# Where the small scale products stand in a shared PSUM tile: behind the first-layer product instead of in front of it

## The chip, the cores and the metric

One core of a Trainium2 chip runs the kernel. The metric is device time in microseconds (us), the median of several runs; lower is better. The engines are TensorE (PE: matmuls; PEld: its weight loads), VectorE (DVE), ScalarE (ACT), GpSimd (POOL) and SyncE (SP), which issues the DMAs. Matmul results land in PSUM, which has eight banks of 512 float32 values for each of 128 partitions.

## The reference

Attention with a mask by hash buckets makes a matrix `x` of 1536 tokens by 512. After that come two feed-forward parts. The change lies in these, so they are what must be seen:

```python
# part 1: four experts, x is 1536x512, w1 4x512x1024, w2 4x1024x512
p = probs / (probs.sum(-1, keepdims=True) + 1e-9)
for e in range(4):
    out += p[:, e:e+1] * (np.maximum(x @ w1[e], 0) @ w2[e])
# part 2: w_in 512x2048, w_out 2048x512
h = out @ w_in
g = np.where(h >= 1, h, np.where(h <= -1, 0, (h + 1) ** 2 / 4))
return g @ w_out
```

The inputs `w_in` and `w_out` are float64; all others are float32.

## The kernel before

**Units, jobs, steps.** The hidden columns of both parts are cut into 12 units `u` of 512: units 0 to 7 are the experts (two units each), 8 to 11 are part 2. A job is a unit with a group of token tiles (128 tokens each), nearly always three tiles, so 384 columns; only the first four jobs of the stage looked at here have two tiles. A job has four steps `f`, one for each 128 of its hidden columns. A step has a first-layer product (`l1b`) and a second-layer part (`l2b`).

The product takes 12 matmuls into columns 0 to `n` (256 or 384) of one PSUM tile `mm`: both operands are split into a high and a low half in float16, and three of the four cross terms are summed over four chunks of 128 (lines 1314 to 1316). The tile fills one bank, and there are two such buffers (tag `m`), so that a buffer comes up again two products later. The second-layer part multiplies the job's tokens, tile by tile, into output tiles `o` (nine matmuls of 512 columns, lines 1341 to 1343), which live in the other six banks, two sets of three. In the fourth step VectorE adds them to `acc` (line 1356 or 1362; in unit 8 ScalarE copies them, line 1360).

**The evictions.** For units 0 to 7 ScalarE reads the product (`gg`, line 1320), makes its high half (`hh`, line 1321), and VectorE makes the low half (`hl`, line 1322). For units 8 to 11 ScalarE reads the product first (`ga`, line 1328), VectorE works on that (line 1329), reads the product again (`gg`, line 1330), ScalarE makes `hh` (line 1331) and VectorE makes `hl` (line 1332).

**The order of the work** in this stage (from about 451 us on) is the order in which the code below issues it. Each engine works off its own queue in that order. The main loop (lines 1427 to 1434) issues the product of job `j + 1`, step `f`, then `step()`, then the second-layer part of job `j`, step `f`, then `step()` again. So the results of a product are used by a second-layer part four steps later. `step()` moves on the side work by one piece each: scans for the largest magnitude of weight tiles (line 1072), the split of weight tiles into halves with their scale (`conv_w`, lines 1191 to 1196), and the bit operations that turn float64 weights into float32 (lines 1137 to 1150). `x_all` (line 1263) rebuilds an input tile in float16 and takes a PSUM tile of tag `m` for itself.

**The riders.** A scale is a power of two from the largest magnitude of a tensor. The largest value has to cross partitions, which TensorE does in two small products (`fin`, line 1078). The first kind, `turn_over`, transposes a column `mx` into one row of 128 (line 1086); VectorE takes the maximum of it (line 1087) and three more operations on single values give `dg` (lines 1088, 1076, 1090). The second kind, `spread`, multiplies `dg` with a row of ones (line 1095), and VectorE copies the result and its reciprocal (lines 1096, 1097). Both use columns 384 to 511 of a PSUM tile that a product uses as well: `rider(ps)` (line 1061) pops at most one of them for each product, when its age (one or two products) is up. Before the change it is called right after the tile is taken, ahead of the product's matmuls.

There are 52 riders, 26 of each kind. In the seven stretches that the rows below are given for, the counts are 3, 29, 8, 8, 2, 2 and 0. The first stretch has the last eight products of 256 columns; the second has the seven units with two jobs each (56 products); each of the five others is one unit with four jobs (16 products): the last expert unit, then units 8 to 11. Three input tiles are rebuilt in the third and nine in the fourth.

Of the kernel before, what the change touches and what calls it, by code (L numbers as in the profile page):

```python
# [285 lines left out]
def attn_moe_kernel(ctx: ExitStack, tc, q, k, v, proj, probs, w1, w2, w_in, w_out, out):  # L286
# [484 lines left out]
    def x_tiles(tt):  # L771
        return x_t[tt // 6], (tt % 6) * 128
# [66 lines left out]
    def l1_mm(j, f, ps, kcs):  # L839
        u, tts = jobs[j]  # L840
        n = 128 * len(tts)
        (xh, xl), c0 = x_tiles(tts[0])
        hi, lo = wt[1][4 * job_load[j] + f]
        for kc in kcs:
            ws = slice(kc * 128, kc * 128 + 128)
            xs = slice(c0, c0 + n)
            pe.matmul(ps[:, 0:n], hi[:, ws], xh[:, kc, xs], start=(kc == 0), stop=False)  # L847
            pe.matmul(ps[:, 0:n], hi[:, ws], xl[:, kc, xs], start=False, stop=False)  # L848
            pe.matmul(ps[:, 0:n], lo[:, ws], xh[:, kc, xs], start=False, stop=(kc == KC - 1))  # L849

    def l1_hi(j, f, ps):
        n = 128 * len(jobs[j][1])
        hts[j, f] = [mode["h"].tile([128, mode["hn"]], F32R, tag=f"h{x}", name=f"h{x}") for x in "hl"]
        act.activation(hts[j, f][0][:, 0:n], ps[:, 0:n], AF.Relu)

    def l1_lo(j, f, ps):
        n = 128 * len(jobs[j][1])
        hh, hl = hts[j, f]
        dve.scalar_tensor_tensor(hl[:, 0:n], ps[:, 0:n], 0.0, hh[:, 0:n].bitcast(F32), ALU.max, ALU.subtract)
# [94 lines left out]
    with tc.manual_schedule():  # L954
# [103 lines left out]
        def mm_tile():  # L1058
            return ps_m.tile([128, 512], F32, tag="m", name="mm")

        def rider(ps):
            for x in pend:
                x[0] -= 1
            if pend and pend[0][0] <= 0:
                pend.pop(0)[1](ps[:, 384:512])
# [161 lines left out]
        def need(kind, u, f):  # L1227
            while (kind, u, f) not in w16:
                got = next(wgen[kind])
                if got is False:  # L1230
                    raise RuntimeError(f"weights {kind} {u} {f} too early")
                if got == "fin" and pend:
                    pend.pop(0)[1](mm_tile()[:, 384:512])
                if got == "w64":
                    next(w64)
# [45 lines left out]
        def scales2(u, c):  # L1281
            if u not in k5:
                k5[u] = t_p.tile([128, 5, 4], F32, tag="k5", name="k5")
            k2, kh, gp, cc, ko = (k5[u][:, i, c] for i in range(5))
            dve.tensor_scalar(k2, e2[:, c], ew[1, u], None, ALU.mult)
            dve.tensor_scalar(kh, k2, 0.5, None, ALU.mult)
            dve.tensor_scalar(gp, k2, 2.0 ** 15, 2.0 ** -15, ALU.mult, ALU.max)
            dve.reciprocal(cc, gp)
            dve.tensor_scalar(ko, gp, ew[2, u], None, ALU.mult)

        def grp(j):
            return jobs[j][1][0] // 3

        def l1b(j, f):
            u, tts = jobs[j]
            n = 128 * len(tts)
            if j >= JF:
                need(1, u, f)
            ps = mm_tile()
            rider(ps)  # L1300
            seen[1].add((j, f))
            if j < JF:
                l1_mm(j, f, ps, range(KC))
                l1_hi(j, f, ps)
                l1_lo(j, f, ps)
                return
            b, c0 = tts[0] // 6, (tts[0] % 6) * 128
            assert all(x_done.count(tt) == (tt >= 6) + (u >= 8) for tt in tts), (j, u, tts, f, x_done, J0, turn)
            xh, xl = x16[b]
            hi, lo = w16[1, u, f]  # L1310
            for kc in range(KC):
                ws = slice(kc * 128, kc * 128 + 128)
                xs = slice(c0, c0 + n)
                pe.matmul(ps[:, 0:n], hi[:, ws], xh[:, kc, xs], start=(kc == 0), stop=False)  # L1314
                pe.matmul(ps[:, 0:n], hi[:, ws], xl[:, kc, xs], start=False, stop=False)  # L1315
                pe.matmul(ps[:, 0:n], lo[:, ws], xh[:, kc, xs], start=False, stop=(kc == KC - 1))  # L1316
            hts[j, f] = hh, hl = [h_p.tile([128, 256], F32R, tag=f"h{y}", name=f"h{y}").bitcast(F16) for y in "hl"]
            gg = g_p.tile([128, 384], F32, tag="gg", name="gg")
            if u < 8:
                act.activation(gg[:, 0:n], ps[:, 0:n], AF.Relu, scale=2.0 ** -15)  # L1320
                act.activation(hh[:, 0:n], gg[:, 0:n], AF.Copy)  # L1321
                dve.tensor_tensor(hl[:, 0:n], gg[:, 0:n], hh[:, 0:n], ALU.subtract)  # L1322
            else:
                if f == 0 and (u == 8 or grp(j) == 0):
                    scales2(u, slice(grp(j), grp(j) + 1) if u == 8 else slice(0, 4))
                k2, kh, gp, cc, ko = (k5[u][:, i, grp(j):grp(j) + 1] for i in range(5))
                a = g_p.tile([128, 384], F32, tag="ga", name="ga")
                act.activation(a[:, 0:n], ps[:, 0:n], AF.Relu, bias=half, scale=kh)  # L1328
                dve.scalar_tensor_tensor(a[:, 0:n], a[:, 0:n], 1.0, a[:, 0:n], ALU.min, ALU.mult)  # L1329
                dve.scalar_tensor_tensor(gg[:, 0:n], ps[:, 0:n], k2, a[:, 0:n], ALU.mult, ALU.max)  # L1330
                act.activation(hh[:, 0:n], gg[:, 0:n], AF.Copy, scale=cc)  # L1331
                dve.scalar_tensor_tensor(hl[:, 0:n], gg[:, 0:n], cc, hh[:, 0:n], ALU.mult, ALU.subtract)  # L1332
# [92 lines left out]
        for f in range(4):  # L1425
            l1b(J0, f)
        for j in range(J0, J1 - 1):
            for f in range(4):
                l1b(j + 1, f)
                if turn and (f or j > JF):  # L1430
                    x_all(*turn.pop(0))
                step()
                l2b(j, f)
                step()
            if jobs[j][0] == LB[NA0]:
                x2q.append(x2_steps(jobs[j][1]))
# [31 lines left out]
```

## Time and profile before

| what | value |
|---|---|
| runs | 1214.49, 1215.84, 1219.51 us; median 1215.84 |
| the profiled execution | 1216.15 us, its span 1214.4 us |
| mean granted clock of TensorE | 0.93 |
| PE, PEld busy | 1024.3 us (84%), 634.8 us (52%) |
| DVE, ACT, POOL busy | 765.3 us (63%), 685.7 us (56%), 287.1 us (24%) |

The span goes from the first to the last instruction of one execution; the rest of the execution's time lies around it. Busy time is the time in which an engine had an instruction of its own at work. Matmuls overlap in their pipeline: one of 512 columns is recorded at some 0.38 us, while the next starts 0.22 us after it, so the distance of starts is what a matmul costs. The granted clock is the share of the full TensorE clock (2.4 GHz) that was granted; it has two levels, 1.0 and 0.5, and other values are means.

### The profile page before, as it was taken

Reading aid. Unit: us, or ns where it says so; the run is one execution under the profiler, and the core shown is the slowest. Engines: PE = TensorE matmul, PEld = TensorE weight load, DVE = VectorE, ACT = ScalarE, POOL = GpSimd, SP = SyncE. Lnnn points to the kernel's source line nnn. Section 1 sums busy time; section 2 is a strip of 40 time slices with the busy share of each in tenths; the row PEclk is TensorE's granted clock in tenths of the full one; section 3 lists DMA queues with packets and bytes.
Section 4 is the critical chain, followed back from the end, with each engine's and each line's share of the span. In section 5 each row is a group of like instructions: output and inputs, shape, how many; then the busy total and the mean of one; then the engine's idle time right before and its main releaser. Section 6 shows DMA issues by size and latency. Waiting matters only on the chain. (4 is left out here: it accounts for less than half of the span.)

```text
span 1214.4 us, 19439 instructions
## 1 busy us (share of the span) xinstructions
PE 1024.3 (84%) x6897; PEld 634.8 (52%) x6897; DVE 765.3 (63%) x2059; ACT 685.7 (56%) x1497; POOL 287.1 (24%) x333
## 2 busy tenths in 40 slices
PE   7589998898999986688778788888877796987998
PEld 3257886686888874344334344444433453443554
DVE  7898888887898565444444543334555666574655
ACT  7888887888788445545445445443543453333332
POOL 0324655345565541101101101120110020000000
PEclk7689999999999988889898889899988999998999
DMA  8999999989999554221312210001100101100002
GB/s 208 209 163 200 214 221 245 212 152 205 188 181 169 126 174 136 70 87 53 104 52 76 61 55 18 1 18 35 35 18 18 35 19 35 35 1 0 1 27 79
DMA packets 252146, 119.40 MB, mean 98 GB/s; under 512 B 180624, under 2 KB 237328, under 8 KB 252048
## 3 DMA queue, kind: packets, MB, share of 16 engines
q1 hardware_dynamic: 249792, 116.84, 42.7%
q10 hardware_dynamic: 2256, 1.31, 0.6%
q8 instruction: 54, 0.88, 0.3%
q14 instruction: 44, 0.36, 0.1%
HBM read 68.19 MB, written 3.15 MB: 59 GB/s over the span
## 5 line engine op out<-in xcount | busy, mean ns | idle before, releaser
L1322 DVE TENSOR_TENSOR hl<-gg,hh 128x384 f16<-128x384 f32 (+1 forms) x80 | 44.6, 557 | 224.1 <-ACT hh L1321 224.1
L683 POOL TENSOR_TENSOR pn<-e,pn 128x192 f16<-128x192 f32 (+3 forms) x157 | 127.9, 819 | 192.7 <-DVE pn L683 54.0
L1320 ACT ACTIVATE gg<-mm 128x384 f32<-128x384 f32 (+1 forms) x80 | 38.3, 478 | 191.1 <-PE mm L1316 191.1
L1314 PE MATMUL mm<-x161h,w1l 128*128 128x384 f16 x192 | 67.6, 352 | 44.8 <-DVE mt L1087 31.5
L1314 PE MATMUL mm<-x161h,w1h 128*128 128x384 f16 x192 | 67.4, 351 | 43.6 <-DVE mt L1087 30.7
L655 DVE CUSTOM_DVE_ANT_0 e<-s,mk,sc 128x768 f32<-128x768 f32 x96 | 96.8, 1008 | 2.7 <-ACT acc L713 1.3
L1331 ACT ACTIVATE hh<-gg,k 128x384 f16<-128x384 f32 x64 | 39.3, 615 | 102.0 <-DVE gg L1330 102.0
L668 ACT ACTIVATE e<-e,usm 128x768 f32<-128x768 f32 x96 | 89.3, 931 | 3.4 <-POOL w1l L833 0.4
L633 PE MATMUL s<-xk,xq 128*128 128x384 f16 (+1 forms) x384 | 83.7, 344 | 8.6 <-DVE usm L655 8.1
L1329 DVE SCALAR_TENSOR_TENSOR ga<-ga 128x384 f32<-128x384 f32 x64 | 40.5, 633 | 75.8 <-ACT ga L1328 75.8
L675 ACT ACTIVATE pn<-e 128x768 f16<-128x768 f32 (+3 forms) x121 | 85.1, 703 | 2.8 <-DMA pt<-pn 2.1
L1328 ACT ACTIVATE ga<-mm,half,k 128x384 f32<-128x384 f32 x64 | 42.5, 665 | 75.4 <-PE mm L1316 66.6
L1341 PE MATMUL o<-w2l,hh 128*128 128x512 f16 x216 | 84.2, 390 | 0.0
L1342 PE MATMUL o<-w2l,hh 128*128 128x512 f16 x216 | 83.5, 386 | 0.0
L847 PE MATMUL m<-x0h,w1h 128*128 128x256 f32 x272 | 83.1, 305 | 0.1
L1343 PE MATMUL o<-w2l,hl 128*128 128x512 f16 x216 | 82.7, 383 | 0.0
L1341 PE MATMUL o<-w2h,hh 128*128 128x512 f16 x208 | 82.4, 396 | 0.0
L1342 PE MATMUL o<-w2h,hh 128*128 128x512 f16 x208 | 81.5, 392 | 0.0
L1343 PE MATMUL o<-w2h,hl 128*128 128x512 f16 x208 | 80.2, 386 | 0.0
L848 PE MATMUL m<-x0l,w1h 128*128 128x256 f32 x272 | 76.8, 283 | 0.0
L849 PE MATMUL m<-x0h,w1l 128*128 128x256 f32 x272 | 76.8, 282 | 0.0
L1315 PEld LDWEIGHTS <-w1h 128*128 128x128 f16 x288 | 29.9, 104 | 88.8 <-issue 73.7
(255 smaller groups left out, 2948.0 us busy)
## 6 DMA issues: line engine op xcount, KB each, us to landing
raw<-in_moe_w_dram SPq DMA_DIRECT2D x123, 256.0 KB, 3.6
r<-in_moe_w_in_dram SPq DMA_DIRECT2D x16, 512.0 KB, 3.8
rawx<-in_moe_w_dram SPq DMA_DIRECT2D x32, 256.0 KB, 4.0
r<-in_moe_w_out_dram SPq DMA_DIRECT2D x16, 512.0 KB, 3.6
out_dram<-acc SPq DMA_DIRECT2D x12, 256.0 KB, 2.1
rk<-in_k_dram SPq DMA_DIRECT2D x5, 384.0 KB, 3.9
rv<-in_v_dram SPq DMA_DIRECT2D x5, 384.0 KB, 4.6
pt<-pn SPq DMA_TRANSPOSE x96, 4.2
```

Of the source, the lines that this page charges most:

```text
L633: pe.matmul(sps[:, j, 0:n], st["xq"][1 - i][:, hh * QG[pgs[m][0]][2] + c], st["x"][:, hh, 384 * j:384 * j + n], start=(i == 0), stop=(i == 1))
L655: dve.tensor_tensor_reduce(out=e.rearrange("p (a b) -> p a b", a=2), in0=u["s"][:, :, 0:384], in1=u["mk"].rearrange("p (a b) -> p a b", a= ...
L668: act.activation(u["e"], u["e"], AF.Exp, scale=-1.0, bias=sm[:, 2:3], accum_out=sm[:, 3:4])
L675: act.activation(u["pn"][:, c0:c1], u["e"][:, c0:c1], AF.Copy)
L683: eng[e].tensor_tensor(u["pn"][:, 768 + c0:768 + c1], u["e"][:, c0:c1], u["pn"][:, c0:c1], ALU.subtract)
L847: pe.matmul(ps[:, 0:n], hi[:, ws], xh[:, kc, xs], start=(kc == 0), stop=False)
L848: pe.matmul(ps[:, 0:n], hi[:, ws], xl[:, kc, xs], start=False, stop=False)
L849: pe.matmul(ps[:, 0:n], lo[:, ws], xh[:, kc, xs], start=False, stop=(kc == KC - 1))
L1314: pe.matmul(ps[:, 0:n], hi[:, ws], xh[:, kc, xs], start=(kc == 0), stop=False)
L1341: pe.matmul(o, hh[:, ts], whi, start=(f == 0), stop=False)
L1342: pe.matmul(o, hh[:, ts], wlo, start=False, stop=False)
L1343: pe.matmul(o, hl[:, ts], whi, start=False, stop=(f == 3))
```

## The change

The call of `rider(ps)` moves from the front of the product to its end. In the branch for the first two jobs of the stage (`j < JF`) it goes between the product and the two evictions; in the general branch it goes behind the loop over `kc` and ahead of the first instruction that evicts the tile.

```diff
             ps = mm_tile()
-            rider(ps)
             seen[1].add((j, f))
             if j < JF:
                 l1_mm(j, f, ps, range(KC))
+                rider(ps)
                 l1_hi(j, f, ps)
                 l1_lo(j, f, ps)
                 return
...
                 pe.matmul(ps[:, 0:n], lo[:, ws], xh[:, kc, xs], start=False, stop=(kc == KC - 1))
+            rider(ps)
             hts[j, f] = hh, hl = [h_p.tile([128, 256], F32R, tag=f"h{y}", name=f"h{y}").bitcast(F16) for y in "hl"]
             gg = g_p.tile([128, 384], F32, tag="gg", name="gg")
```

## Rows read from the trace of the kernel before

**Rows 1.** The page, part 1: busy time, share of the span, instructions.

```profile
PE 1024.3 (84%) x6897; PEld 634.8 (52%) x6897; DVE 765.3 (63%) x2059; ACT 685.7 (56%) x1497; POOL 287.1 (24%) x333
```

**Rows 2.** Waits of PE over the span: us in total, times, longest.

```profile
PE mm L1314 <- DVE mt L1087: 73.7, 26, 5.9
PE mm L1314 <- DVE sw L1097: 30.0, 22, 4.3
...
PE mm L1314 <- DVE gg L1330: 9.1, 6, 4.0
...
PE mm L1086 <- DVE mx L1083: 7.9, 5, 2.6
...
PE mm L1314 <- DVE s L1097: 7.0, 4, 2.2
```

**Rows 3.** Instruction groups, 500 to 1215 us: count | busy us, mean ns | idle before.

```profile
L776 PE MATMUL mm<-ident,acc 128*128 128x128 f32 x48 | 8.7, 312 | 0.0
```

**Rows 4.** Seven stretches: length, PE, PEld, DVE, ACT, POOL busy, granted clock, DMA.

```profile
451.30:492.90 41.60, 26.77 (x159) 18.78 (x159) 25.77 (x55) 22.72 (x55) 4.95 (x5) 0.89 0.51 150
492.90:805.00 312.10, 250.99 (x1193) 124.85 (x1193) 138.83 (x338) 149.66 (x322) 38.00 (x32) 0.89 0.18 55
805.00:884.40 79.40, 69.28 (x356) 35.83 (x356) 37.13 (x90) 35.07 (x73) 8.21 (x8) 0.96 0.09 28
884.40:984.80 100.40, 76.88 (x382) 40.35 (x380) 58.42 (x140) 43.58 (x80) 9.50 (x8) 0.92 0.07 22
984.80:1064.60 79.80, 67.08 (x339) 34.25 (x338) 51.18 (x95) 34.14 (x61) 9.42 (x7) 0.94 0.11 33
1064.60:1140.30 75.70, 65.83 (x340) 33.56 (x338) 47.31 (x89) 29.02 (x50) 6.95 (x6) 0.95 0.00 1
1140.30:1202.60 62.30, 62.30 (x338) 32.90 (x337) 36.99 (x66) 20.47 (x32) 0.00 (x0) 1.00 0.07 26
```

**Rows 5.** Timeline around a first-kind rider: start us, us, engine line, [idle before <-releaser].

```profile
600.93 0.27 PE L1086 MATMUL mm<-ident,mx 128*1 128x128 f32 x1
...
601.35 2.06 DVE L1356 SCALAR_TENSOR_TENSOR acc<-o,prk,acc 128x512 f32<-128x512 f32 x3
...
603.66 0.27 DVE L1087 TENSOR_REDUCE mt<-mm 1x1 f32<-1x128 f32 x1
...
603.98 0.48 PE L1314 MATMUL mm<-x161h,w1h 128*128 128x384 f16 x1 [2.78 <-DVE mt L1087]
...
604.26 0.52 PE L1315 MATMUL mm<-x161l,w1h 128*128 128x384 f16 x1
...
604.58 0.52 PE L1316 MATMUL mm<-x161h,w1h 128*128 128x384 f16 x1
```

**Rows 6.** Timeline around a second-kind rider, and the conversions that use its result.

```profile
613.30 0.17 PE L1095 MATMUL mm<-dg,ones 1*128 1x1 bf16 x1
...
613.97 0.32 PE L1314 MATMUL mm<-x161h,w1h 128*128 128x384 f16 x1 [0.49 <-DVE sw L1097]
...
615.91 0.38 PE L1341 MATMUL o<-w2h,hh 128*128 128x512 f16 x1
...
616.11 0.49 ACT L1320 ACTIVATE gg<-mm 128x384 f32<-128x384 f32 x1 [2.38 <-PE mm L1316]
...
616.63 0.53 ACT L1321 ACTIVATE hh<-gg 128x384 f16<-128x384 f32 x1
...
617.07 1.32 ACT L1191 ACTIVATE w1h<-raw,sw 128x512 f16<-128x512 f32 x2
...
617.80 0.75 DVE L1192 SCALAR_TENSOR_TENSOR w1h<-raw,sw,w1h 128x512 f16<-128x512 f32 x1
```

**Rows 7.** Instruction groups of ACT from 884.4 to 984.8 us.

```profile
L1331 ACT ACTIVATE hh<-gg,k 128x384 f16<-128x384 f32 x15 | 9.2, 614 | 19.3 <-DVE gg L1330 19.3
```

**Rows 8.** Instruction groups of DVE from 984.8 to 1064.6 us.

```profile
L1332 DVE SCALAR_TENSOR_TENSOR hl<-gg,k,hh 128x384 f16<-128x384 f32 x15 | 9.3, 619 | 10.3 <-ACT hh L1331 10.3
```

**Rows 9.** Waits of PE from 451.3 to 493.1 us.

```profile
PE mm L1314 <- DVE mt L1087: 9.3, 2, 5.6
...
PE mm L1314 <- DVE sw L1097: 1.2, 1, 1.2
```

## The prediction

> **What bounds the kernel now.** I read the page's busy times first: TensorE is busy for 84% of the span, no other engine for more than 63% [rows 1]. So TensorE is nearest to the bound, and the question is what it idles for. The list of its waits answers that [rows 2]: the first matmul of a first-layer product waits 26 times, 73.7 us in all, for VectorE's maximum over a transposed column (line 1087, the read of the first kind of rider), and 26 times, 30.0 + 7.0 = 37.0 us, for the reciprocal of line 1097, the last read of the second kind. That is every one of the 52 riders, 110.7 us, 2.13 us each (2.83 and 1.42 by kind). The riders themselves wait another 7.9 us for their input (line 1083). Every other wait of a product, for `gg` on line 1330, is 9.1 us.
>
> The timeline shows why [rows 5]. The transpose starts at 600.93 and takes 0.27 us. VectorE has three output updates of 2.06 us and another small step still ahead, and reaches the read only at 603.66. The product, which writes other columns of the same tile, starts at 603.98, after a wait of 2.78 us. Its matmuls are then 0.32 us apart (604.26 to 604.58), against 62.3 us for 16 products and 16 second-layer parts in the last full stretch. That stretch has no rider, no idle TensorE and a granted clock of 1.00, the 2.4 GHz level, while the stretches with riders show 0.89 to 0.96 [rows 4]: after an idle stretch part of the work goes at the 1.2 GHz level. So a rider costs its wait and some clock behind it.
>
> **The change, part by part.** A rider's instructions are one weight load and one matmul on TensorE and four or two small VectorE instructions; no DMA, nothing on ScalarE, GpSimd or SyncE. Their number and their order among riders stay, as does their place in VectorE's queue: ahead of this tile's `hl`, behind what was there. On TensorE they go behind the product's 12 matmuls, and what follows them is the second-layer part, which writes other banks. That removes the 110.7 us. The next first-layer product uses the other buffer of the two; the rider's own comes up again at the product after that.
>
> *The price of a step without a rider's wait.* 62.3 / 16 = 3.89 us [rows 4]. The product is 615.91 - 613.97 = 1.94 of it [rows 6], the second-layer part 1.95. A rider's own matmul takes 0.27 or 0.17 us, mean 0.22 [rows 5, 6]. An input tile's rebuild adds four transposes: 8.7 us for 12 tiles, 0.72 each [rows 3].
>
> *What the moved read does to its tile.* Cover: from the product's end to the next use of its bank lie 1.95 + 3.89 = 5.8 us. VectorE's lag behind a transpose is at most 5.9 us (the longest wait, rows 2); the rider now comes 1.94 us later on TensorE, so at worst the read ends 4.0 us behind the product's end. ScalarE's eviction, 0.49 us [rows 6], fits behind it even then, with 1.3 us left. Whether that eviction must wait for VectorE's read at all, no row of before shows: there the two reads lie on either side of the product. Bounds: nothing, if reads of one tile need no order; 4.0 us per rider on ScalarE if they do. It can't be a gain, since the eviction starts directly at the product's end now (616.11, rows 6). I take about 1.5 us, the mean lag of the first kind beyond the product with the read itself (2.83 - 1.94 + 0.27 = 1.2) rounded up, and the cover hides it. If the cover goes, a rider shows the part above 5.8 us.
> The Trainium skill, "PSUM — Partial Sum Buffer", section "PSUM bank collisions raise a hardware error", wants any two engines kept apart on one bank, reads against reads included, which speaks against this change. By it the eviction does wait for VectorE's read. No run here shows it yet, and the sum is the same either way while the cover holds.
>
> *The chain that the second kind feeds.* Its reciprocal now comes 1.94 us later, less the wait saved. The conversions that use it stand in ScalarE's queue behind this tile's eviction and `hh`: 616.11, 616.63, then 617.07, and the low half starts on VectorE at 617.80 and takes 0.75, done 2.7 us after the product's end [rows 6]. Its user is the product two steps on, 5.8 us after that end. So 3.1 us are left; a held eviction of 1.5 us still fits. What VectorE has queued behind a rider is `hl` of this tile, which waits for `hh` anyway and is read four steps later.
>
> *The sum by stretch* [rows 4], now to after:
> 1. 451.3:492.9, eight narrow products, 3 riders: their waits go, 9.3 + 1.2 us [rows 9]: 41.6 to 31.
> 2. 492.9:805.0, 56 products, 29 riders: 56 x 3.89 = 218, riders 6.4, and 8 us that I keep for new waits at bursts: 312.1 to 232.5. VectorE (139) and ScalarE (150 us) have room in it.
> 3. 805.0:884.4, 16 products, 8 riders, 3 rebuilds: 62.3 + 1.8 + 2.2: 79.4 to 66.3.
> 4. 884.4:984.8, 16 products, 8 riders, 9 rebuilds. TensorE: 62.3 + 1.8 + 6.5 = 70.6. Here ScalarE binds as well: it must sit between `ga` and `hh` while VectorE makes `gg`, 19.3 / 15 = 1.29 us a product [rows 7]; 43.6 busy + 16 x 1.29 = 64, and some short waits for other VectorE results. Each rider adds its read and its way there, some 0.7 us, to that loop if evictions are held: 70.6 + 5.6, 100.4 to 76.
> 5. 984.8:1064.6, 2 riders: TensorE 62.7; VectorE 51.2 busy + 10.3 in which it must sit for `hh` [rows 8] = 61.5. Two engines at the same level don't mesh fully; 3 us more: 79.8 to 66.
> 6. 1064.6:1140.3, 2 riders: 62.7 and some 2 us of the waits for `gg`: 75.7 to 64.5.
> 7. 1140.3:1202.6: unchanged, 62.3.
> Together 751.3 to 598.6, 152.7 us less. The profiled execution took 1216.15 us (span 1214.4); 1216.15 - 152.7 = 1063.4, and the median of the runs is 0.3 us below that execution: 1063 us. A second count agrees: 110.7 us of waits, some 8 of the riders' own, and the clock. The granted clock of stretches 1 to 6 lies below 1.00 by 59 us of time in sum; about two thirds of that fall on matmuls, 40 us: 159.
> What is late next is TensorE's own work in the first part and the ScalarE-VectorE loop after 884.
>
> **The rivals.** (a) The lag of VectorE comes back as a wait for the bank. For it: VectorE loses the rests that the stalls gave it, and in stretches 4 and 5 it and ScalarE are nearly full. Against: 5.8 us of cover, and both engines under 70% in stretch 2. If each of the 26 first-kind riders still costs 2 us, it is 1063 + 52 = 1115.
> (b) The clock isn't given back: the waits go, the 40 us stay: about 1100. Against it, the last stretch has the same turns through the two banks at 1.00 [rows 4].
> The Trainium skill, "TensorE: Matmul & The Clock Gate", section "A second HAM failure mode: psum-queue depth-cycling", says that small idles while cycling through banks can make the clock swing; here that would be this rival.
> (c) The product was late for another reason that the rider's wait covers, converted weights above all, and so the change does not do what it says. Then little moves, 1190 to 1216. Against: in the step of rows 6 the weights are 3.1 us early, and waits under other names are few [rows 2].
> (d) Slower: the held eviction. ScalarE stops at the rider's tile until VectorE has caught up, VectorE then stops for `hh`, and that lag is in front of the next rider. If nothing hides it, each rider costs its wait now (2.13) + read 0.27 [rows 5] + eviction 0.49 + `hh` 0.53 [rows 6] = 3.42 us, 178 in all: 1063 + 178 = 1241. It decides from 152.7 / 52 = 2.94 us per rider on. Against: the two products' work between a bank's uses.
>
> **How the numbers follow.** Forecast 0.68 (own range 1042 to 1085: the lower end is TensorE's own work alone, 31 + 224 + 66 + 71 + 63 + 63 + 62 = 580 for the seven stretches, so 1045, and 3 us for the scatter of runs; at the upper end 11 first-kind riders keep 2 us each); (a) 0.20; (b) 0.05; (c) 0.03; (d) 0.04. The range goes from 1045 to 1118, which takes in (b) and the centre of (a) and leaves out the rest. About half a per cent, 6 us, is what can be told from no change: faster 0.94, same 0.02, slower 0.04.
>
> **What would show it.** Right: the waits of line 1314 for lines 1087 and 1097 are gone; 56 products in some 230 us; the granted clock at 0.98 or more from 490 on; the wait of `gg` on line 1320 ends at VectorE's read on rider tiles, if reads are kept apart. Wrong: new waits of line 1314 for `gg` (line 1320 or 1330) of tens of us; line 1086 waiting for line 1083 behind the product as before; a second-layer matmul or a product waiting for weights (lines 1192, 1196).

## The result, and the profile after

The changed kernel takes 1066.39 us (median; 1065.43 to 1067.28), the one before 1215.16 us beside it (1212.97 to 1219.51): ratio 0.8772, 95% interval 0.8746 to 0.8798. The forecast was 1063 us with a range of 1045 to 1118. The profiled execution has a span of 1063.3 us, 151.1 less than before, and a mean granted clock of 0.976 where it was 0.93. All times here are medians of undisturbed executions; one of experiment 9's four, at 2512 us, is left out.

In the changed kernel the lines from 1320 to 1362 stand one further down (the eviction `gg` is line 1321, the reading of `ga` 1329 to 1331, `hh` 1332, `hl` 1323 or 1333, the second-layer part 1342 to 1344). The first view is the page of after, part 1 (the row that answers to [rows 1]) and the clock row of part 2 (the span in 40 slices, in tenths of full speed), with the clock row of the page of before as the last line.

```profile
PE 974.7 (92%) x6897; PEld 618.3 (58%) x6897; DVE 765.9 (72%) x2059; ACT 681.9 (64%) x1497; POOL 287.1 (27%) x333
...
PEclk9779999989999999999999999999999999999999
...
PEclk7689999999999988889898889899988999998999
```

The instructions are the same ones and VectorE and ScalarE are busy for as long as before; TensorE's 49.6 us less of busy time, with the same 6897 matmuls, is nearly all the clock: the second half of the span has nines only, where before it had eights among them. The next view is the list of TensorE's waits over the span of after, the answer to [rows 2] (us in total, times, longest).

```profile
PE mm L1314 <- DVE gg L1331: 22.6, 19, 4.0
...
PE mm L1314 <- ACT gg L1321: 5.6, 3, 3.3
...
PE mm L1086 <- DVE mx L1083: 0.9, 2, 0.6
...
PE mm L1314 <- ACT w1h L1191: 0.3, 1, 0.3
```

Before, there were two more waits of this kind beside those of [rows 2]:

```profile
PE mm L1314 <- ACT gg L1320: 3.3, 1, 3.3
...
PE mm L1086 <- ACT gg L1320: 1.1, 1, 1.1
```

Both waits for riders (lines 1087 and 1097, 110.7 us) are gone, and so is nearly all of what the riders themselves waited for (7.9 + 1.1 to 0.9 us). The products' waits for a bank (`gg`) grew from 9.1 + 3.3 = 12.4 to 22.6 + 5.6 = 28.2 us. Waits of the products and riders come to 132.4 us before and 29.4 after (0.3 us for weights in each), 103.0 us of the 151.1. The rest is the clock. The seven stretches of [rows 4] are, in the changed kernel (length, busy us of PE, PEld, DVE, ACT, POOL, granted clock, DMA share and GB/s):

```profile
451.00:479.40 28.40, 23.92 (x155) 17.37 (x153) 19.30 (x44) 19.30 (x47) 4.71 (x4) 0.94 0.62 187
479.40:700.60 221.20, 220.12 (x1194) 115.27 (x1193) 142.17 (x343) 149.92 (x329) 36.88 (x31) 1.00 0.26 79
700.60:765.70 65.10, 65.10 (x358) 34.65 (x357) 39.55 (x96) 34.58 (x73) 9.48 (x8) 1.00 0.14 41
765.70:844.30 78.60, 69.30 (x381) 36.86 (x380) 58.95 (x140) 42.78 (x80) 8.48 (x7) 1.00 0.09 28
844.30:919.30 75.00, 65.74 (x339) 33.44 (x338) 52.77 (x98) 34.63 (x62) 10.58 (x8) 0.98 0.12 36
919.30:989.20 69.90, 64.92 (x338) 33.45 (x338) 47.27 (x89) 29.29 (x50) 6.94 (x6) 0.98 0.00 1
989.20:1051.50 62.30, 62.30 (x338) 32.88 (x336) 36.98 (x66) 20.46 (x32) 0.00 (x0) 1.00 0.07 26
```

TensorE's busy time in the seven stretches sums to 571.4 us here and to 619.1 in [rows 4]: the same matmuls go 47.7 us faster, which with the 103.0 us of waits makes up the 150.8 us by which the stretches are shorter. (Length times what the granted clock lacks to 1.00 sums to some 5 us here, against 59 in [rows 4]; of these 54 us some 6 lay on idle time, which is in the waits already.) In stretch 2 TensorE has an instruction at work for 220.12 of 221.20 us. The stretches from 765.7 on, except the last, are where it still idles: 9.3, 9.3 and 5.0 us.

How a rider runs now is seen in a first-kind one of stretch 2, the timeline of after (start us, us, engine line, [idle before <- releaser]; the answer to [rows 5]).

```profile
575.20 0.33 PE L1316 MATMUL mm<-x161h,w1l 128*128 128x384 f16 x1
...
575.37 0.27 PE L1086 MATMUL mm<-ident,mx 128*1 128x128 f32 x1
...
575.48 0.38 PE L1342 MATMUL o<-w2h,hh 128*128 128x512 f16 x1
...
575.71 2.06 DVE L1357 SCALAR_TENSOR_TENSOR acc<-o,prk,acc 128x512 f32<-128x512 f32 x3
...
578.68 0.27 DVE L1087 TENSOR_REDUCE mt<-mm 1x1 f32<-1x128 f32 x1
...
578.99 0.49 ACT L1321 ACTIVATE gg<-mm 128x384 f32<-128x384 f32 x1 [3.70 <-DVE mt L1087]
...
581.31 0.33 PE L1314 MATMUL mm<-x161h,w1l 128*128 128x384 f16 x1
```

The transpose starts 0.17 us behind the last matmul of the product, and the second-layer part 0.11 us behind the transpose. VectorE still has its output updates ahead of the read and ends it 3.6 us behind the product's end; the eviction starts 0.04 us later and is over at 579.48, 1.8 us ahead of the next use of this buffer, at 581.31. VectorE is still late, 3.6 us from the transpose's start to the read's end (3.0 in [rows 5]); now TensorE has 5.9 us of other work before it needs the bank.

### The profile page after: what moved, and what is told of

Read it like the earlier page. It is cut to its first block, busy times and chain, and to the rows that moved or that the text cites. A ratio compares the mean times of both kernels' runs of the same rounds, so it can differ in the third digit from the quotient of the medians.

```text
span 1063.3 us, 19398 instructions
## 1 busy us (share of the span) xinstructions
PE 974.7 (92%) x6897; PEld 618.3 (58%) x6897; DVE 765.9 (72%) x2059; ACT 681.9 (64%) x1497; POOL 287.1 (27%) x333
## 5 line engine op out<-in xcount | busy, mean ns | idle before, releaser
L633 PE MATMUL s<-xk,xq 128*128 128x384 f16 (+1 forms) x384 | 82.3, 339 | 10.8 <-DVE usm L655 9.9
L1342 PE MATMUL o<-w2l,hh 128*128 128x512 f16 x216 | 82.2, 381 | 0.0
L1343 PE MATMUL o<-w2l,hh 128*128 128x512 f16 x216 | 82.1, 380 | 0.0
L1342 PE MATMUL o<-w2h,hh 128*128 128x512 f16 x208 | 79.0, 380 | 0.0
L1343 PE MATMUL o<-w2h,hh 128*128 128x512 f16 x208 | 78.8, 379 | 0.0
L1333 DVE SCALAR_TENSOR_TENSOR hl<-gg,k,hh 128x384 f16<-128x384 f32 x64 | 39.6, 619 | 44.6 <-ACT hh L1332 44.6
L1344 PEld LDWEIGHTS <-hl 128*128 128x128 f16 x424 | 41.5, 98 | 50.2 <-issue 0.3
L1314 PE MATMUL mm<-x161h,w1h 128*128 128x384 f16 x192 | 62.6, 326 | 5.1 <-DVE gg L1331 4.0
```

Of the source, the lines that this page charges most:

```text
L633: pe.matmul(sps[:, j, 0:n], st["xq"][1 - i][:, hh * QG[pgs[m][0]][2] + c], st["x"][:, hh, 384 * j:384 * j + n], start=(i == 0), stop=(i == 1))
L1342: pe.matmul(o, hh[:, ts], whi, start=(f == 0), stop=False)
L1343: pe.matmul(o, hh[:, ts], wlo, start=False, stop=False)
L1344: pe.matmul(o, hl[:, ts], whi, start=False, stop=(f == 3))
```

## The experiments

Theory A, that of the prediction: what cost the time was that the product wrote a tile in which VectorE still had a read to do. Rival B: the place of a small matmul ahead of the product in TensorE's order costs it. For what is left after the change, theory C: the eviction held by VectorE's read is hidden, but close to its cover. The rival that came up on the way, D: ScalarE's queue, held at one instruction, makes VectorE later still (its `hl` waits for ScalarE's `hh`, and the next read stands behind that), and so multiplies each delay.

**1 and 2. One kind of rider moved alone.** The count of ages goes on as before; one kind is issued in front, the other behind the product. The first experiment has the first kind behind, the second one the second kind (`turn_over` in place of `spread` in the condition).

```diff
-        def rider(ps):
-            for x in pend:
-                x[0] -= 1
-            if pend and pend[0][0] <= 0:
+        def rider(ps, front):
+            if front:
+                for x in pend:
+                    x[0] -= 1
+            if pend and pend[0][0] <= 0 and front == (pend[0][1].__name__ == "spread"):
                 pend.pop(0)[1](ps[:, 384:512])
+                return True
+            return False
...
             ps = mm_tile()
-            rider(ps)
+            gone = rider(ps, True)
...
+            gone or rider(ps, False)
```

> Only the first kind of rider (the transpose, line 1086) goes behind the product; the second kind (the spread) stays in front. Shared-tile theory: the 73.7 us of its waits, some 8 us of its own wait for its input and some 30 us of clock go, the 37 us of the second kind stay: about 1105 us (1095 to 1115), and the product still waits for line 1097's read 26 times and never for line 1087's. Rival, the gain is per rider whatever its kind (26 of 52): about 1141.

> Only the second kind (the spread) goes behind the product; the transpose stays in front. Shared-tile theory: 37 us of waits and some 8 us of clock go: about 1170 us (1160 to 1180). Per-rider rival: about 1141.

The first took 1132.6 us (ratio 0.9295, 0.9257 to 0.9332), the second 1177.23 us (0.9684, 0.9647 to 0.9722). The waits of TensorE, with the first kind behind:

```profile
PE mm L1318 <- DVE sw L1100: 49.4, 22, 5.8
...
PE mm L1318 <- DVE s L1100: 9.8, 4, 3.0
```

and with the second kind behind:

```profile
PE mm L1318 <- DVE mt L1090: 74.6, 26, 5.9
```

Each move takes away the waits of its own kind. The second experiment came out as expected; the first missed by 28 us, 22 of them because the second kind's waits (line 1097, here 1100) didn't stay at 37.0 us but grew to 59.2. VectorE is later at the second kind's read than before. That it lost the rest which the first kind's waits gave it is one reading; that evictions are held now (39.2 us of ScalarE's time in this run) is another, and no run tells the two apart. Against 1216.19 us measured beside them, the gains of the two are 83.6 and 39.0 us, 122.6 together, while both moves at once bring 149: such waits don't add up.

**3. In front, but in a tile of its own.** The riders stay ahead of the product and take a turn of the two buffers for themselves.

```diff
-                pend.pop(0)[1](ps[:, 384:512])
+                pend.pop(0)[1](mm_tile()[:, 384:512])
...
+            rider()
             ps = mm_tile()
-            rider(ps)
```

> All riders stay in front of the product in TensorE's order, but a rider takes a turn of the two buffers for itself, so that the product goes into the other one. Shared-tile theory: the product has nothing to wait for but the eviction of the product before it, which for the expert units ends some 0.7 us behind that product and so inside the second-layer part; nearly all of the gain comes: about 1080 us (1070 to 1100), what is missing being the riders' own wait for line 1083 and waits for the eviction in units 8 to 11. Rival, the gain comes from the place in TensorE's order: 1200 to 1215.

It took 1078.86 us (0.887, 0.8853 to 0.8887), as A has it. Two stretches of it, the second and the fourth:

```profile
481.80:702.60 220.80, 220.15 (x1193) 115.10 (x1192) 140.14 (x340) 149.58 (x325) 36.91 (x31) 1.00 0.26 78
768.60:856.50 87.90, 72.51 (x381) 38.41 (x380) 58.97 (x141) 43.88 (x81) 9.18 (x8) 0.96 0.08 25
```

Stretch 2 is as short as after the change, 220.8 us, with the riders in front: B is out, and the shared tile is the cause. Of the 12 us that it loses to the change, 9 lie in stretch 4 (87.9 against 78.6 us). TensorE waits there for the low half of rebuilt input tiles (line 1271, 6.2 us), for the riders' own input (4.0 us) and for a buffer in which a rider's result is still unread (2.2 us); how much of that comes from the turn that a rider takes wasn't tested.

**4. VectorE later.** To see how near the cover is to its end, three additions on a scratch tile (2.1 us) go ahead of each first-kind read.

```diff
                 pe.transpose(ps[0:1], mx, ident)
+                for _ in range(3):
+                    dve.tensor_tensor(pad, pad, pad, ALU.add)
                 dve.tensor_reduce(mt, ps[0:1], AX.X, ALU.max)
```

> The changed kernel with three more VectorE additions (128x512, some 0.69 us each, 2.1 us) ahead of the read of each first-kind rider. Cover theory: 5.8 us lie between a product's end and the next use of its tile, so the units 0 to 7 lose nothing (their 56 products stay at some 221 us); units 8 to 10, where VectorE binds, lose up to 6 x 2.1 = 12 us: 1067 to 1080 us. Rival, a held eviction is passed on to TensorE: 26 x 2.1 = 55 us, about 1120.

It took 1100.25 us (0.9045, 0.9031 to 0.9058), 34 us more than the changed kernel, and missed both values. Stretch 2 went from 221.2 to 239.1 us. The stretch, and one rider of it in the timeline:

```profile
483.00:722.10 239.10, 223.54 (x1195) 115.61 (x1194) 175.42 (x386) 148.45 (x328) 37.92 (x31) 0.99 0.24 74
...
588.40 0.27 PE L1086 MATMUL mm<-ident,mx 128*1 128x128 f32 x1
...
593.30 2.13 DVE L1088 TENSOR_TENSOR pad<-pad 128x512 f32<-128x512 f32 x3
...
595.36 0.27 DVE L1089 TENSOR_REDUCE mt<-mm 1x1 f32<-1x128 f32 x1
...
595.66 0.49 ACT L1325 ACTIVATE gg<-mm 128x384 f32<-128x384 f32 x1 [5.76 <-DVE mt L1089]
...
596.20 0.32 PE L1318 MATMUL mm<-x161h,w1l 128*128 128x384 f16 x1 [1.70 <-ACT gg L1325]
```

The read ends 7.2 us behind the product's end, the eviction at 596.15, and the next use of the bank waits 1.70 us for it. Over the 15 first-kind riders of stretch 2 the read's mean distance from the product's end went from 2.4 to 5.9 us, by 3.5 us for 2.1 us of work. So something multiplies the delay.

**5 and 6. The read behind the eviction.** If it is the held eviction, VectorE's reads can be issued behind the eviction, while the rider's matmul stays where the change put it; experiment 6 does that with the three additions of 4.

```diff
+        reads = []
+        def finish_reads():
+            while reads:
+                reads.pop(0)()
...
             def turn_over(ps):
                 pe.transpose(ps[0:1], mx, ident)
-                dve.tensor_reduce(mt, ps[0:1], AX.X, ALU.max)
...
+                reads.append(lambda: read_max(ps))
...
                 dve.scalar_tensor_tensor(hl[:, 0:n], gg[:, 0:n], cc, hh[:, 0:n], ALU.mult, ALU.subtract)
+            finish_reads()
```

> As the changed kernel, but only the rider's matmul stands ahead of the eviction; VectorE's reads of it (lines 1087 to 1090, or 1096 and 1097) are issued behind the tile's last eviction instruction (in the first step of units 8 to 11 they stay ahead). Theory, the eviction that is held by the read is hidden in the expert units and paid only in units 8 to 11: the 56 products stay at 221 us, unit 8 (78.6 us) loses a few; 1058 to 1066 us, and ScalarE's waits for lines 1087 and 1097 are gone. Rival, the held eviction costs nothing anywhere: same time as the changed kernel, 1066.

> The same, with three more VectorE additions (2.1 us) ahead of each first-kind read, as in the earlier run that took 1100 us. Theory, that run lost its time because a held eviction makes VectorE late for the next one (the lag feeds on itself): with the reads behind the eviction the 56 products go back to 221 to 226 us and the whole to 1062 to 1078. Rival, 2.1 us more of VectorE work per rider is simply too much for it, wherever it stands: 1090 to 1100.

They took 1070.31 us (0.8799, 0.8773 to 0.8824) and 1104.25 us (0.9084, 0.9056 to 0.9113). Without the additions nothing is gained in all. Stretch 2 is 220.0 us in place of 221.2, so the held evictions of the changed kernel cost at most that much there, which is C. In stretch 4 this version is slower (82.3 against 78.6 us): there the product now waits for the late read itself.

```profile
PE mm L1328 <- DVE mt L1092: 5.9, 3, 3.0
```

So whether the held evictions cost time in units 8 to 10 stays open. With the additions the order alone did not help, and the theory that the eviction held by the read is all that multiplies the delay fell, though stretch 2 is 232.1 us, 7 less than in 4. The stretch in 6, and what ScalarE does ahead of such an eviction:

```profile
482.80:714.90 232.10, 221.52 (x1194) 114.76 (x1193) 169.49 (x385) 149.44 (x329) 37.59 (x31) 1.00 0.25 76
...
555.36 0.68 DVE L1166 TENSOR_TENSOR w<-t,m 128x512 f32<-128x512 f32 x1
...
556.07 0.63 ACT L1078 ACTIVATE jw<-w 128x512 bf16<-128x512 f32 x1 [4.42 <-DVE w L1166]
...
556.70 0.47 ACT L1341 ACTIVATE gg<-mm 128x384 f32<-128x384 f32 x1
```

It stands at another instruction, the scan of a weight tile converted from float64 (line 1072 of the changed kernel), which waits 4.42 us for VectorE's last operation on that tile (line 1150) with the eviction queued behind it. These waits are 38.0 us in the changed kernel and 78.4 us here.

**7. Less conversion.** What do the conversions cost in all? Five of the seven VectorE operations on each float64 tile are left out, so the converted weights hold other values.

```diff
-                dve.tensor_scalar(t, mi, 3, None, ALU.logical_shift_left)
...
-                dve.tensor_tensor(wv, t.bitcast(F32), m, ALU.add)
+                dve.tensor_tensor(wv, m, m, ALU.add)
```

> The changed kernel with five of the seven VectorE operations of each float64 weight tile left out (the values are then not those of the reference). Theory, what is left of waits in units 8 to 10 is the VectorE-ScalarE loop with these operations in it: unit 9 goes from 75.0 to about 65, unit 10 from 69.9 to 64, unit 8 from 78.6 to 74; the whole to 1046 (1040 to 1053). Rival, the loop is bound by ScalarE's weight halves: 1060 or more.

It took 1045.48 us (0.8612, 0.8578 to 0.8647), as expected; unit 9 stayed 4.5 us above its 65. Its stretches 4 to 6:

```profile
758.10:832.80 74.70, 69.30 (x382) 36.89 (x381) 48.83 (x117) 43.45 (x82) 8.56 (x8) 1.00 0.11 35
832.80:902.30 69.50, 64.66 (x339) 33.35 (x338) 42.60 (x76) 35.39 (x64) 8.97 (x8) 0.98 0.10 31
902.30:966.30 64.00, 63.07 (x339) 32.96 (x338) 41.76 (x78) 28.16 (x48) 6.96 (x6) 1.00 0.00 1
```

They are 3.9, 5.5 and 5.9 us shorter than after the change, and TensorE's idle time in them falls from 23.6 to 11.2 us. VectorE's conversion work, in bursts between the operations of an eviction, is about half of what is left there.

**8. The scan one step later.** The scan of a converted tile is issued with the first operations of the next one.

```diff
                 yield
+                scan_todo()
                 dve.tensor_scalar(t, mi, 3, None, ALU.logical_shift_left)
...
-                scan(wv, am64[kind, u][:, f:f + 1])
-                w64_t[key] = wv
+                todo.append((key, wv, am64[kind, u][:, f:f + 1]))
```

> The changed kernel with the scan of a converted float64 weight tile on ScalarE issued one step later, so that ScalarE does not stop for VectorE's last operation on it (38 us of such waits over the span, some 12 of them in units 8 to 10). Theory, ScalarE's stops are part of the loop in units 8 to 10: 1058 to 1064 us. Rival, VectorE alone binds there: 1066.

1061.12 us (0.8734, 0.8708 to 0.876), 0.5% under the changed kernel, with intervals that overlap, so no gain is shown. Stretch 5 of its trace is 71.9 us in place of 75.0.

**9 and 12. Both holds away, with the late reads.** The kernel of 6 with the scan of 8, run twice; the stretches are from the second run.

> The run with the reads behind the eviction and 2.1 us more of VectorE work per first-kind rider (1104 us, 232.1 us for the 56 products), and also the scan of a converted float64 tile one step later, so that ScalarE's evictions stand behind neither. Theory, ScalarE stopping for a late VectorE (first by the rider's read, then by the scan) is what turns 2.1 us into more: the 56 products go to 220 to 224 us and the whole to 1080 to 1092. Rival, VectorE's own queue is too long around the fourth step, whatever ScalarE does: the 56 products stay at 230 or more, the whole at 1095 or more.

> The same kernel as the version with the rider's reads behind the eviction, three more VectorE additions ahead of each first-kind read and the scan of a converted tile one step later, taken once more for a trace of stretch 2 (the 56 products). If ScalarE's holds are what turned 2.1 us of VectorE work per rider into 18 us of stretch 2 (221.2 to 239.1 us), the stretch without either hold is 220 to 225 us, and ScalarE's wait at the scan (78.4 us in the version that still had it) is under 25 us; the total is 1079 to 1084 us. If VectorE's own work is enough for it, stretch 2 stays at 230 us or more, and the gain of the whole (1104 to 1082 us) lies in the stretches behind it.

1082.25 us (0.8904, 0.887 to 0.8937) and 1079.85 us (0.8883, 0.8868 to 0.8898), against 1104.25 us with the scan's hold, as the theory has it both times. Stretch 2 in the second of the two:

```profile
478.30:698.30 220.00, 219.96 (x1194) 115.23 (x1193) 169.84 (x385) 150.46 (x327) 37.66 (x31) 1.00 0.26 80
```

and what ScalarE still waits at the scan in it:

```profile
ACT jw L1078 <- DVE w L1175: 6.7, 5, 3.9
```

The same 2.1 us of additions ahead of each first-kind read cost 18 us of stretch 2 in 4, 11 in 6, and nothing here: VectorE carries 169.84 us of work in 220.00 and TensorE never idles. D is shown for stretch 2: with both holds away, the late reads cost nothing there. Which share the scan's hold has where the read is still ahead of the eviction wasn't run.

In the whole they still cost some 19 us (1079.85 against the 1061.12 of 8), and most of that lies in stretch 4, 93.1 against 79.8 us. There the product waits for the late reads themselves:

```profile
PE mm L1342 <- DVE mt L1094: 16.9, 7, 5.1
```

12.5 us of these lie in stretch 4. In unit 8 the rival of 6 fits: so much VectorE work ahead of a read is too much, with or without ScalarE's holds.

**10 and 11. A version that uses 8.** 10 is 8 with one thing more: the five small VectorE operations that make an input tile's scales in part 2 (`scales2`) go to the end of the step before, so that `ga` need not wait for them. 11 converts the float64 tiles at double pace in stretch 3's unit besides, to empty the later units.

```diff
-                if f == 0 and (u == 8 or grp(j) == 0):
-                    scales2(u, slice(grp(j), grp(j) + 1) if u == 8 else slice(0, 4))
...
+            if f == 3 and j + 1 < J1:
+                u = jobs[j + 1][0]
+                if u >= 8 and (u == 8 or grp(j + 1) == 0):
+                    scales2(u, slice(grp(j + 1), grp(j + 1) + 1) if u == 8 else slice(0, 4))
```

```diff
             w64_step()
+            if quick:
+                w64_step()
...
+            quick[:] = [1] * (jobs[j + 1][0] == LB[NA0])
```

> The changed kernel with the scan one step later (1061 us alone) and with the five small VectorE operations of a unit's activation scales (lines 1285 to 1289) issued at the end of the step before, so that the first eviction of a job does not stop for them (8.5 us of such waits in units 8 to 10). Theory, ScalarE's stops are part of the loop in units 8 to 10: 1053 to 1060 us. Rival, VectorE alone binds: 1061, no change.

> The same, and the float64 conversion runs at twice the pace during the last expert unit, where VectorE has some 25 us to spare, so that unit 8 has less of it. Theory, conversion work in unit 8 is what it loses (4 us by the run that left most of it out): 1050 to 1057 us, unit 7 stays at 65 to 67 us. Rival, the work only moves: the same as without.

10 took 1058.24 us (0.8711, 0.8685 to 0.8737), 0.8% under the changed kernel; 11 took 1056.93 us (0.8713, 0.8684 to 0.8742), the same. Both intervals lie just below that of the changed kernel, but not clear of 8, so what the scales alone bring isn't shown. In 11 stretches 5 and 6 are shorter than in 10 (68.8 and 63.2 us in place of 71.4 and 68.3), but stretch 4 is longer by as much as 4.6 us and stretch 3 by 1.9: the work moved, it didn't go.

## Why the prediction was right, and where its terms were not

**The waits.** The 110.7 us are gone, as forecast; experiment 3 shows that the shared tile made them. The forecast took "every other wait of a product" to be the 9.1 us for line 1330; 3.3 us for line 1320 stood beside them. Nor do the two kinds have separate prices: with the first kind's waits alone gone, the second kind's grew from 37.0 to 59.2 us (experiment 1).

**The clock.** The second count had 40 us for it, two thirds of what the clock lacked; 47.7 came back on matmuls, nearly nine tenths of the 54 us by which the clock columns differ. With 110.7 us of riders' waits, 8.1 of the riders' own and 15.8 less for bank waits that grew, that gives the 150.7 measured, where the second count had 159. Rival (b) is out: with the same turns through two banks the granted clock is 1.00 in stretches 2 to 4.
By the Trainium skill, "TensorE: Matmul & The Clock Gate", section "A second HAM failure mode: psum-queue depth-cycling", small idles between groups could have kept it swinging. That is hardly seen here: stretches 5 and 6, with 13 waits of 14.2 us for `gg`, show 0.98, and stretch 4, with 8.4 us of them, 1.00.

**The sum by stretch.** Forecast 31, 232.5, 66.3, 76, 66, 64.5, 62.3; measured (from first product to first product) 29.0, 221.2, 65.1, 78.6, 75.0, 69.9, 62.3. The sum was 2.5 us too low, but as a balance: 14.5 us too careful in the first three, 17.0 us too hopeful in units 8 to 10. That the total came so near is luck in this part.

*Too careful:* stretch 2. The 8 us kept for bursts weren't needed, and a rider costs TensorE 0.12 us ((221.2 - 56 x 3.89) / 29) in place of 0.22, since the next matmul starts 0.11 us behind it.

*Too hopeful:* "3 us more" for the meshing of two engines in unit 9 and "some 2 us of the waits for `gg`" in unit 10; they are 12.3 and 7.2 us above the 62.7 of TensorE's own work. (Unit 8 is 2.6 us above its 76.) What stands there, from the timeline of after in unit 10:

```profile
924.77 0.69 DVE L1141 SCALAR_TENSOR_TENSOR t<-m,t 128x512 int32<-128x512 int32 x1
925.38 2.06 DVE L1363 SCALAR_TENSOR_TENSOR acc<-o,k,acc 128x512 f32<-128x512 f32 x3
927.35 0.42 DVE L1143 TENSOR_SCALAR m<-t 128x512 int32<-128x512 int32 x1
927.68 0.23 DVE L1285 TENSOR_SCALAR k<-e,ew 128x4 f32<-128x4 f32 x1
...
928.21 0.67 ACT L1329 ACTIVATE ga<-mm,half,k 128x384 f32<-128x384 f32 x1 [2.67 <-DVE k L1287]
...
929.51 0.62 DVE L1331 SCALAR_TENSOR_TENSOR gg<-mm,k,ga 128x384 f32<-128x384 f32 x1
...
930.18 0.48 PE L1314 MATMUL mm<-x160h,w1h 128*128 128x384 f16 x1 [2.52 <-DVE gg L1331]
```

Two conversion operations, the output updates and the small scale operations stand ahead of what ScalarE needs for `ga`; ScalarE idles 2.67 us, `gg` ends at 930.13 and TensorE has waited 2.52 us for the bank. Mean loads of 68% and 42% on VectorE and ScalarE in this stretch don't show that; the order within a burst does. Experiments 7, 8 and 10 took 5.5, 3.1 and 3.6 us off stretch 5, in one trace each, by removing or moving such work. What the other microseconds of that loop are wasn't settled.

**The cover.** 5.8 us lie between a product's end and the next use of its bank, as read. "At worst 4.0 us" for the read's end was broken twice in stretch 2, at its start (5.3 and 4.3 us), and the first of these made the next product wait 1.1 us; the other first-kind reads of it end at most 3.6 us behind. In stretch 5 one ends 4.2 us behind. That the next use has room was right, but experiment 4 shows how little: 2.1 us more work ahead of each first-kind read, and the bank is late.

**The held eviction.** It is held, which no row of before could tell. ScalarE's waits of after:

```profile
ACT gg L1321 <- DVE mt L1087: 39.0, 17, 4.3
ACT jw L1072 <- DVE w L1150: 38.0, 26, 4.0
ACT gg L1321 <- DVE sw L1097: 20.5, 15, 3.3
...
ACT ga L1329 <- DVE mt L1087: 4.9, 3, 2.1
...
ACT ga L1329 <- DVE s L1097: 2.1, 1, 2.1
```

These and two smaller rows for the second kind (1.1 us at `gg`, 0.9 at `ga`) are 68.5 us over 39 of the riders, 1.8 us each and 1.3 over all 52. 1.5 had been taken, but by a sum that counts the read's 0.27 us twice: the wait of 2.83 us ends with the read and holds it already (603.66 to 603.93, then 603.98, in [rows 5]). The price of rival (d) has the same slip. In stretch 2, experiment 5 shows that the hold costs at most 1.2 us while the cover lasts.
The Trainium skill, "PSUM — Partial Sum Buffer", section "PSUM bank collisions raise a hardware error", has any two engines kept apart on one bank, two readers of different columns too. By these rows the kernel keeps that order, since the eviction of columns 0 to 383 starts directly behind VectorE's read of column 384 and on; what would come of breaking it no run here shows.

**The other rivals.** (a) came true for 16 us, by which the waits for `gg` grew (12.4 to 28.2): 22.6 us of these lie in units 8 to 10, with 12 riders in all, and 5.6 in the first two stretches, not 2 us at each rider. (c) is out: the products' wait for weights is 0.3 us. The loop of (d) exists: experiment 4 shows it in stretch 2, and 12, without ScalarE's holds, shows stretch 2 free of it. In the changed kernel the cover is long enough to keep it from starting there.

## What to carry to other kernels

A small product that borrows columns of a large product's PSUM tile belongs behind the large one where, as here, other work lies before the tile's next use: that work then covers the slow reader, where in front the reader's whole lag stands on TensorE. Measure how much of the cover is used by making the reader later on purpose, and look at each in-order queue for an instruction that waits with an eviction behind it; here it multiplied the delay. A sum of waits isn't a sum of gains: taking away one kind of wait made the other kind longer.

## What was not expected of the hardware

A matmul with little work behind a long product is nearly free: the transpose is recorded at 0.27 us, but the next matmul starts 0.11 us after it. And queues that work in order can make a delay grow: in experiment 4, 2.1 us of work on VectorE ahead of a read moved its end by 3.5 us on the mean of stretch 2.
